# Expert blocks turned by 16-bit DMA transposes in place of TensorE transposes, in a Fourier-filter and top-2 mixture-of-experts kernel

## The chip, the cores and the metric

The kernel runs on one core of a Trainium2 chip. The metric is the time of one execution on the device in microseconds (us): the median of several runs, beside one execution that the hardware profiler recorded. TensorE is called PE in the profile, its weight loads PEld, VectorE DVE, ScalarE ACT, GpSimd POOL and SyncE SP. SP and POOL issue the DMAs.

## The reference

```python
X = np.fft.rfft(x, axis=1)                       # x: 8 x 2496 x 256
y = np.fft.irfft(X * (filt_r + 1j * filt_i)[None], n=2496, axis=1)
x = y.reshape(19968, 256)
noisy = x @ w_gate + np.log1p(np.exp(x @ w_noise)) * noise      # 8 experts
top2 = np.argpartition(-noisy, 2, axis=1)[:, :2]
top2_w = softmax over the two chosen values (sum + 1e-9 below)
for e in range(8):
    for k in range(2):
        mask = top2[:, k] == e
        h = np.maximum(x[mask] @ w1[e], 0.0)     # w1: 8 x 256 x 1024
        out[mask] += top2_w[mask, k, None] * (h @ w2[e])    # w2: 8 x 1024 x 256
```

So a filter over the sequence by Fourier transform, and on its result a mixture of eight experts in which each of the 19968 rows goes to two of them.

## The kernel before

**Stages.** The Fourier part (`fft_stream`) works batch by batch and channel half by channel half with small matrix products. For each half, `i2` (L507) takes the filtered rows from PSUM with one ACT copy (L525) and writes them to the DRAM tensor `y`, 256 values and 8 gate weights (264 32-bit words) a row. `gate` and `slots` choose the experts, and `route` writes lists of row numbers per expert to DRAM.

**Blocks.** The expert part (`expert`, L1070) takes those rows in blocks of one expert. The constants give 16 single blocks of 512 rows (2 after the first batch, 10 more after the second, 4 more after the third), then 24 pairs of 512-row blocks that share their weights, then 7 single blocks of 512, 14 of 256 and 4 of 128: 71 blocks of 512 and 18 small ones. `ready` is the number of batches whose rows a block may hold, so it is 1 for the first two blocks and above 1 for all others.

**One block.** `gather` (L988) has POOL fetch 128 rows at a time from `y` by an indirect DMA into a slot `xg`; there are 8 slots, two 512-row blocks, in the tile `stage`. `turn` (L1001) transposes them on PE: for each half `kc` of the 256 channels up to four 128x128 transposes (L1010) into one PSUM bank `xps`; ACT then copies the bank, rounded, to `mxh` (L1014) and DVE subtracts that from the bank to give the rest, `mxl` (L1015). POOL copies the block's gate weights out of the same slots (L1019). The first layer runs over eight tiles `f` of 128 hidden units, each from six 128x512 matmuls (L122 to L124: high x high, high x low, low x high for both `kc`); the PSUM bank of every third tile is one of `yps`, of the others one of `hps`. ACT applies relu with rounding to `hh` (L1097), DVE makes the rest `hl` (L1098). The second layer goes over the block's quarters `t` of 128 rows (L1122, L1123; earlier blocks L122 to L124 with yps), ACT and DVE scale the result with the gate into one of six slots `yo` (L1127, L1129), and POOL adds it to `out` with an indirect DMA (L1130).

**Weights.** `front` (L969) starts a new expert's block: `load_w` has SP load the eight pieces of w1 and w2 into four slots `wst`, and `wsplit` (L1059 on ACT, L1060 on DVE) splits each into high and low parts. `front` ends with `turn` for its block.

**Order.** Two blocks are held in `ahead`, gathered early by `fetch` (L1063). The next block's `turn` or `front` is written between the first and the second layer of the present block; after each step `run` lets the Fourier stream make some steps, by a table of paces (`PACE`). A scheduler orders the instructions of each engine by a simulated timeline, so that the layers of two blocks and the Fourier products are interleaved; each engine then takes its queue in order. `pin` holds some instructions to the written order, and `after` puts one behind another.

Of the kernel before, what the change touches and what calls it, by code (L numbers as in the profile page):

```python
# [10 lines left out]
F32 = mybir.dt.float32  # L11
R32 = mybir.dt.float32r
F16 = mybir.dt.float16
I32 = mybir.dt.int32
AF = mybir.ActivationFunctionType
ALU = mybir.AluOpType
AX = mybir.AxisListType
# [5 lines left out]
NG = 22  # L23
# [103 lines left out]
def f32v(ap):  # L127
    return ap.bitcast(F32)
# [14 lines left out]
class Moe:  # L143
    def __init__(self, ctx, tc, io):
        self.tc, self.nc, self.io = tc, tc.nc, io
        nc = self.nc
        self.cp = ctx.enter_context(tc.tile_pool(name="cp", bufs=1))
        self.dp = ctx.enter_context(tc.tile_pool(name="dp", bufs=1, space=DRAM))
        self.y = self.dp.tile([NROW, YW], F32, name="y")
# [33 lines left out]
    def setup(self):  # L183
# [12 lines left out]
        self.sgn = cp.tile([64, 20], F32, name="sgn")  # L196


        self.stage = cp.tile([128, 2048 + 8 * YW + 1536], F32, name="stage")
# [29 lines left out]

    def slot(self, nm):  # L230

        at, n, w = {"wst": (0, 4, 512), "xg": (2048, 8, YW), "yo": (2048 + 8 * YW, 6, 256)}[nm]
        i = self.turns[nm] = (self.turns.get(nm, -1) + 1) % n
        return self.stage[:, at + w * i:at + w * i + w]

# [42 lines left out]
    def init_dram(self):  # L278
        nc, io = self.nc, self.io
        z = self.z  # L280

        nc.sync.dma_start(self.lst.rearrange("(n r) c -> n (r c)", r=4), io["empty"].to_broadcast([NLR // 4, 4 * LR]))
        for a, w in (self.y, YW), (io["out"], D):
# [168 lines left out]
    def logits(self, r):  # L452
        nc, P = self.nc, self.P
        if r == 0:
            self.uh = P.tile([120, 24, 16], R32, name="uh")
# [51 lines left out]
    def i2(self, n, g0):  # L507
        nc, P, h = self.nc, self.P, n % 2
        Dh, Dl = self.cD
        th, tl = self.t3t.pop((n, g0))  # L510
        k = min(4, NG - g0)
        m = 128 * k
        p = self.ps("q6")
        if tl is None:
            nc.tensor.matmul(p[:RP, :m], self.rD, th[:120, :m], start=True, stop=True)  # L515
        else:
            nc.tensor.matmul(p[:RP, :m], Dh, th[:120, :m], start=True, stop=False)
            nc.tensor.matmul(p[:RP, :m], Dh, tl[:120, :m], start=False, stop=False)
            nc.tensor.matmul(p[:RP, :m], Dl, th[:120, :m], start=False, stop=True)
# [5 lines left out]
        nc.scalar.copy(yt[:, :k, :128], p[:RP, :m].rearrange("p (g d) -> p g d", g=k))  # L525
# [3 lines left out]
        nc.sync.dma_start(y[:, g0:g0 + k, h * 128:h * 128 + w], yt[:, :k, :w])  # L529

    def fft_stream(self):

# [185 lines left out]
    def gate(self, bt, lgp):  # L718
# [30 lines left out]

        m, c, oh = [], [], []  # L750
        for i in range(2):
            mi, ci, oi = t(f"m{i}", [RP, NG]), t(f"c{i}", [RP, NG]), t(f"oh{i}")
# [213 lines left out]
        nc.gpsimd.tensor_copy(ids, t)  # L966
        return ids, n, nt, s, self.tabs[i]

    def front(self, blk, xg, fill=None):  # L969


        nc = self.nc
        lt, n, nt, s, tabi, ready = blk
        with self.after(self.spw):
            re = nc.sync.value_load(tabi[0:1, 1, s:s + 1], min_val=0, max_val=E - 1)
        self.ra = nc.gpsimd.value_load(tabi[0:1, 1, s:s + 1], min_val=0, max_val=E - 1)
# [5 lines left out]
        if fill and self.held_any:  # L982
            xT = self.pin(self.turn, xg, nt, hold=False, only=[self.nc.tensor.engine])
        else:
            xT = self.turn(xg, nt)
        return w1, xT, w2st

    def gather(self, blk, i):  # L988

        lt, n, nt, s, tabi, ready = blk  # L990
        xg = []
        for t in range(nt):
            x = self.slot("xg")
            self.pin(lambda: self.nc.gpsimd.indirect_dma_start(  # L994
                out=x, out_offset=None, in_=self.y[:BLK + ready * ROWS],
                in_offset=bass.IndirectOffsetOnAxis(ap=lt[:, i, t:t + 1], axis=0)),
                hold=False, only=[self.nc.gpsimd.engine])
            xg.append(x)
        return xg, self.turns["xg"] + 1 - nt

    def turn(self, xg, nt):  # L1001

        nc, P = self.nc, self.P
        xT = []
        xg, at = xg
        w = 128 * nt
        for kc in range(2):
            q = self.PS.tile([128, 512], F32, name="xps", bufs=1)
            for t in range(nt):
                nc.tensor.transpose(q[:, t * 128:(t + 1) * 128], xg[t][:, kc * 128:(kc + 1) * 128], self.ident)  # L1010
            h = P.tile([128, 512], R32, name=f"mxh{kc}", bufs=1)
            l = P.tile([128, 512], R32, name=f"mxl{kc}", bufs=1)
            h, l = h[:, :w], l[:, :w]
            nc.scalar.copy(h, q[:, :w])  # L1014
            nc.vector.tensor_sub(l, q[:, :w], f32v(h))  # L1015
            xT.append((h, l))
        gate = P.tile([128, 4, 1], F32, name="gt", bufs=3)[:, :nt]
        rows = self.stage[:, 2048:2048 + 8 * YW].rearrange("p (s w) -> p s w", w=YW)[:, at:at + nt, D:]
        nc.gpsimd.tensor_copy(gate, rows[:, :, bass.ds(self.ra, 1)])  # L1019
        xT.append(gate)  # L1020
        return xT

    def load_w(self, re, nm, nt):
# [39 lines left out]
    def fetch(self, may):  # L1063

        if len(self.ahead) < 2 and may():
            p = next(self.parts, None)
            if p is not None:
                self.ahead.append((*p, self.gather(*p)))

    def expert(self, parts, may, fill=None):  # L1070

        nc, P = self.nc, self.P
        self.parts, self.ahead = parts, []
        self.fetch(lambda: True)
        cur = None
        while self.ahead:
            blk, i, xg = self.ahead.pop(0)
            lt, n, nt, s, tabi, ready = blk
            w = 128 * nt
            if cur is None:  # L1080
                cur = self.front(blk, xg, fill)
            w1, xT, w2st = cur
            if i == 0:
                w2, adds = [], []
            ids, gate = lt[:, i], xT[2]
            self.fetch(may)
            hh = []
            for f in range(8):

                p = self.PS.tile([128, 512], F32, name="hps", tag="hps" if f % 3 < 2 else "yps", bufs=2)[:, :w]  # L1090
                for kc in range(2):
                    wh, wl = w1[f // 2]
                    o = (f % 2) * 128
# [1 line left out]
                h = P.tile([128, 512], R32, name="hh", bufs=8)[:, :w]  # L1095
                l = P.tile([128, 512], R32, name="hl", bufs=8)[:, :w]
                nc.scalar.activation(h, p, AF.Relu)  # L1097
                nc.vector.scalar_tensor_tensor(l, p, 0.0, f32v(h), op0=ALU.max, op1=ALU.subtract)  # L1098
# [5 lines left out]
            if late:  # L1104
                self.fetch(lambda: True)
            if self.ahead:
                b2, i2, x2 = self.ahead[0]
                cur = (w1, self.turn(x2, nt), None) if i2 else self.front(b2, x2, fill if late else None)
            self.fetch(may)
            yield  # L1110
            for t in range(nt):
# [135 lines left out]
```

## Time and profile before

| | us |
|---|---|
| median of 3 runs | 2302.6 |
| lowest and highest | 2300.22, 2303.27 |
| the profiled execution | 2311.56 |
| its span, first to last instruction | 2309.8 |

The mean granted TensorE clock of the profiled execution was 0.940. Indirect gathers (128 rows of `y` each) took a median of 2.9 us from issue to landing, the scatters 4.2 us. In all 332.80 MB were moved at a mean of 144 GB/s.

In the profile's rows, a group is a line, engine and operation with its tiles; behind the bar stand its busy time, the mean time of one in ns, and how long the engine was idle ahead of it, with what ended that. A row of the timeline is the start, the duration and the instruction; "x4" says that four were merged, and the duration is then that of all. A row of the stages is a stretch of the span with the busy time of each engine in it. A row of waits says who waited for whom: total us, times, longest.

### The profile page before, as it was taken

The numbers are of one execution on the slowest core, as the hardware profiler recorded it, in microseconds if no ns is written. First come the engines' busy times: TensorE is split into PE (matmuls) and PEld (weight loads), VectorE is DVE, ScalarE is ACT, GpSimd is POOL, SyncE is SP. The second block draws the span as 40 slices with busy tenths as digits, with TensorE's granted clock in tenths as the row PEclk, the third lists the DMA queues.
The fourth block names the chain that finished last, engine by engine and source line by source line (L and its number), as shares of the span: only waits on it lengthen the run. The fifth ranks groups of instructions, "written<-read, shape, count | busy, mean of one in ns | idle before, by whom it ended". The sixth has DMA issues, their size and how long they took to land.

```text
span 2309.8 us, 39448 instructions
## 1 busy us (share of the span) xinstructions
PE 2267.6 (98%) x13087; PEld 1898.6 (82%) x13087; DVE 1544.5 (67%) x3356; ACT 1193.7 (52%) x2385; POOL 925.1 (40%) x821
## 2 busy tenths in 40 slices
PE   8889999999999999999999999999999999999998
PEld 6548888888888788887888888888888888889997
DVE  4767788678779665875659655964444444657886
ACT  5655655555664554444544444444434444546775
POOL 4014244334234333443344433435454444444442
PEclk8889999999999999999999999999999999999998
DMA  8686757657765655454544554444444444658774
GB/s 233 181 255 167 184 147 202 170 157 177 192 168 131 148 131 124 102 144 118 117 115 105 138 141 85 90 99 89 97 91 90 89 99 104 149 138 232 218 214 131
DMA packets 286296, 332.80 MB, mean 144 GB/s; under 512 B 37532, under 2 KB 197252, under 8 KB 286084
## 3 DMA queue, kind: packets, MB, share of 16 engines
q1 hardware_dynamic: 224771, 245.80, 35.4%
q0 software_dynamic: 61312, 84.40, 21.9%
q8 instruction: 105, 1.72, 0.3%
q14 instruction: 108, 0.88, 0.1%
HBM read 225.63 MB, written 105.25 MB: 143 GB/s over the span
## 4 chain that ended last, share of the span: by engine, by line
PE 93%; DVE 2%; DMA 2%; ACT 1%; issue 1%; SPq 0%; POOL 0%; POOLq 0%; DVEq 0%; ACTq 0%
PE yps L1122 20%; PE hps L122 13%; PE hps L123 12%; PE hps L124 12%; PE yps L1123 10%; PE xps L1010 3%; PE q L429 3%; PE yps L124 2%; PE yps L122 2%; PE yps L123 2%; PE q L493 2%; PE u L440 1%; PE q L318 1%; PE q L515 1%; PE q L390 1%
## 5 line engine op out<-in xcount | busy, mean ns | idle before, releaser
L1122 PE MATMUL yps<-w,hh 128*128 128x512 f32 x2016 | 715.3, 399 | 0.6 <-DVE stage L1129 0.6
L1130 POOL DMA_INDIRECT out<-stage,ids x316 | 524.6, 1660 | 274.2 <-DVE stage L1129 109.8
L994 POOL DMA_INDIRECT stage<-y,ids x316 | 325.3, 1029 | 665.3 <-PE xps L1010 276.0
L1123 PE MATMUL yps<-w,hl 128*128 128x256 f32 x2016 | 547.2, 281 | 0.2 <-DVE hl L1098 0.2
L123 PE MATMUL hps<-mxl,w1h 128*128 128x512 f32 (+2 forms) x1424 | 534.0, 376 | 0.0
L1098 DVE SCALAR_TENSOR_TENSOR hl<-hps,hh 128x512 fp32r<-128x512 f32 (+2 forms) x712 | 435.8, 626 | 143.4 <-ACT hh L1097 141.6
L124 PE MATMUL hps<-mxh,w1l 128*128 128x512 f32 (+2 forms) x1424 | 526.7, 371 | 0.0
L122 PE MATMUL hps<-mxh,w1h 128*128 128x512 f32 (+2 forms) x1424 | 524.6, 378 | 0.9 <-DVE hl L1098 0.8
L1097 ACT ACTIVATE hh<-hps 128x512 fp32r<-128x512 f32 (+2 forms) x712 | 378.9, 550 | 237.0 <-PE hps L124 226.9
L1122 PEld LDWEIGHTS yps<-w,hh 128*128 128x128 f32 x2016 | 372.3, 188 | 78.4 <-DVE stage L1129 0.9
L1123 PEld LDWEIGHTS yps<-w,hl 128*128 128x128 f32 x2016 | 379.6, 189 | 18.7 <-DVE mxl L1015 1.2
L124 PEld LDWEIGHTS hps<-mxh,w1l 128*128 128x128 f32 x1424 | 268.6, 189 | 45.6
L122 PEld LDWEIGHTS hps<-mxh,w1h 128*128 128x128 f32 x1424 | 265.4, 188 | 48.9 <-DVE hl L1098 2.9
L123 PEld LDWEIGHTS hps<-mxl,w1h 128*128 128x128 f32 x1424 | 268.6, 189 | 40.5 <-issue 0.3
L1127 ACT ACTIVATE stage<-yps,gt 128x256 f32<-128x256 f32 x316 | 142.5, 476 | 268.9 <-PE yps L1123 242.7
L1129 DVE SCALAR_TENSOR_TENSOR stage<-yps,gt,stage 128x256 f32<-128x256 f32 x252 | 115.4, 479 | 177.3 <-ACT stage L1127 177.0
L1015 DVE TENSOR_TENSOR mxl<-xps,mxh 128x512 fp32r<-128x512 f32 (+2 forms) x178 | 112.1, 630 | 147.4 <-ACT mxh L1014 144.9
L1014 ACT CAST mxh<-xps 128x512 fp32r<-128x512 f32 (+2 forms) x178 | 95.8, 538 | 220.3 <-PE xps L1010 186.9
L1059 ACT CAST w1h<-stage 128x512 fp32r<-128x512 f32 x188 | 116.7, 621 | 93.0 <-PE hps L123 56.6
L1060 DVE TENSOR_TENSOR w1l<-stage,w1h 128x512 fp32r<-128x512 f32 x188 | 129.1, 687 | 45.1 <-ACT w1h L1059 44.4
L1060 DVE TENSOR_TENSOR w<-stage,w 128x512 fp32r<-128x512 f32 x224 | 147.0, 685 | 15.0 <-ACT w L1059 14.7
L122 PE MATMUL yps<-w,hh 128*128 128x256 f32 x512 | 146.8, 289 | 2.6 <-ACT hh L1097 2.6
(222 smaller groups left out, 3067.8 us busy)
## 6 DMA issues: line engine op xcount, KB each, us to landing
stage<-w SPq DMA_DIRECT2D x412, 256.0 KB
x<-x SPq DMA_DIRECT2D x88, 256.0 KB
fd<-c SPq DMA_DIRECT2D x77, 240.0 KB
wb<-w SPq DMA_DIRECT2D x18, 1024.0 KB
fx<-fd SPq DMA_DIRECT2D x140, 128.0 KB
out<-z SPq DMA_DIRECT2D x24, 702.0 KB
y<-yt SPq DMA_DIRECT2D x40, 248.6 KB
y<-yt SPq DMA_DIRECT2D x40, 234.0 KB
```

Source lines behind the costliest of these rows:

```text
L122: nc.tensor.matmul(o, lh, rh, start=start, stop=False)
L123: nc.tensor.matmul(o, lh, rl, start=False, stop=False)
L124: nc.tensor.matmul(o, ll, rh, start=False, stop=stop)
L994: self.pin(lambda: self.nc.gpsimd.indirect_dma_start(out=x, out_offset=None, in_=self.y[:BLK + ready * ROWS], in_offset=bass.IndirectOffse ...
L1059: nc.scalar.copy(h, sv)
L1060: nc.vector.tensor_sub(l, sv, f32v(h))
L1097: nc.scalar.activation(h, p, AF.Relu)
L1098: nc.vector.scalar_tensor_tensor(l, p, 0.0, f32v(h), op0=ALU.max, op1=ALU.subtract)
L1122: nc.tensor.matmul(bank, h, hl, start=(f == 0), stop=False)
L1123: nc.tensor.matmul(p, l, hl[:, 0], start=False, stop=(f == 7))
L1127: nc.scalar.activation(o, p, AF.Copy, scale=gate[:, t])
L1130: a = nc.gpsimd.indirect_dma_start(out=self.io["out"][:BLK + ready * ROWS], out_offset=bass.IndirectOffsetOnAxis(ap=ids[:, t:t + 1], axis= ...
```

## The change

`y` becomes an integer tensor of the same size. The ACT copy in `i2` now splits each 32-bit value into its two 16-bit halves, so that within each 128 channels a row of `y` holds 128 low halves and then 128 high halves. Gate weights stay as they are.

512-row blocks with `ready` above 1 are turned by DMA: `flip` issues one `dma_start_transpose` from SP for each 128 gathered rows, 128 x 512 halves, into one tile `xt` (one buffer), and then has POOL copy the gate weights (`take`). Only one turned block stands at a time; the next one's `flip` comes at the end of the present one's `turn` or right behind its gather. `turn` then has DVE join the two halves of each channel (a copy of 1024 16-bit elements for each `kc`) into a 32-bit slot `x32`, ordered behind the fifth tile's subtraction of L1098; ACT's `mxh` and DVE's `mxl` are made from that slot.

All other blocks are turned on PE as before, with an ACT copy ahead that joins the halves from the `xg` slots into `x32`.

To make room, `xg` has 4 slots in place of 8, `yo` 4 in place of 6; `uh` and `oh` share buffers with `ut0` and `gl`. For blocks that are turned by DMA, every third tile of the first layer takes the bank `xps` in place of one of `yps`. `fetch` at the start of a block is only called if the next one is turned, or fewer than four slots are held. The core of the diff:

```diff
-        at, n, w = {"wst": (0, 4, 512), "xg": (2048, 8, YW), "yo": (2048 + 8 * YW, 6, 256)}[nm]
+        at, n, w = {"wst": (0, 4, 512), "xg": (2048, 4, YW), "yo": (2048 + 4 * YW, 4, 256), "x32": (3072 + 4 * YW, 2, 512)}[nm]
...
-        nc.scalar.copy(yt[:, :k, :128], p[:RP, :m].rearrange("p (g d) -> p g d", g=k))
+        nc.scalar.copy(yt.bitcast(U16)[:, :k, :256].rearrange("p g (two d) -> p g two d", two=2),
+                       p.bitcast(U16)[:RP, :2 * m].rearrange("p (g d two) -> p g two d", g=k, two=2))
...
+    def by_dma(self, ent):
+        return ent[0][2] == BLK // 128 and ent[0][5] > 1
+
+    def take(self, ent):
+        xg, at, ra = ent[2]
+        gate = self.P.tile([128, 4, 1], F32, name="gt", bufs=3)[:, :len(xg)]
+        self.nc.gpsimd.tensor_copy(gate, self.picked(ent)[:, :, D:][:, :, bass.ds(ra, 1)])
+        return gate
+
+    def flip(self):
+        ent = next((e for e in self.ahead if not e[3]), None)
+        if ent is None or not self.by_dma(ent) or self.standing:
+            return
+        self.standing = True
+        xt = self.P.tile([128, 4, 512], U16, name="xt", bufs=1)
+        for t, x in enumerate(ent[2][0]):
+            self.nc.sync.dma_start_transpose(xt[:, :, 128 * t:128 * t + 128], x.bitcast(U16)[:, :2 * D])
+        ent[3] = xt, self.take(ent)
...
-    def turn(self, xg, nt):
+    def turn(self, ent):
...
+        if self.by_dma(ent):
+            self.flip()
+        q, xT = [], []
         for kc in range(2):
-            q = self.PS.tile([128, 512], F32, name="xps", bufs=1)
-            for t in range(nt):
-                nc.tensor.transpose(q[:, t * 128:(t + 1) * 128], xg[t][:, kc * 128:(kc + 1) * 128], self.ident)
...
+            x = self.slot("x32")[:, :w]
+            xu = x.bitcast(U16)
+            if ent[3]:
+                with self.after(self.early_l):
+                    nc.vector.tensor_copy(xu.rearrange("p (t two) -> p two t", two=2), ent[3][0][:, 2 * kc:2 * kc + 2])
+            else:
+                nc.scalar.copy(xu.rearrange("p (t d two) -> p t d two", t=nt, two=2),
+                               self.picked(ent).bitcast(U16)[:, :, 256 * kc:256 * kc + 256].rearrange("p t (two d) -> p t d two", two=2))
+            q.append(x)
+        for kc in range(2):
+            x = q[kc]
+            if not ent[3]:
+                x = self.PS.tile([128, 512], F32, name="xps", bufs=1)[:, :w]
+                for t in range(nt):
+                    nc.tensor.transpose(x[:, t * 128:(t + 1) * 128], q[kc][:, t * 128:(t + 1) * 128], self.ident)
+            h = P.tile([128, 512], R32, name=f"mxh{kc}", bufs=1)[:, :w]
+            l = P.tile([128, 512], R32, name=f"mxl{kc}", bufs=1)[:, :w]
+            nc.scalar.copy(h, x)
+            nc.vector.tensor_sub(l, x, f32v(h))
+            xT.append((h, l))
...
+        self.flip()
         return xT
...
-            self.fetch(may)
+            if not self.ahead or self.ahead[0][3] or sum(len(a[2][0]) for a in self.ahead) < 4:
+                self.fetch(may)
+            third = ("xps", 1) if self.by_dma(ent) else ("yps", 2)
...
-                p = self.PS.tile([128, 512], F32, name="hps", tag="hps" if f % 3 < 2 else "yps", bufs=2)[:, :w]
+                tag, bufs = ("hps", 2) if f % 3 < 2 else third
+                p = self.PS.tile([128, 512], F32, name="hps", tag=tag, bufs=bufs)[:, :w]
...
+                v = nc.vector.scalar_tensor_tensor(l, p, 0.0, f32v(h), op0=ALU.max, op1=ALU.subtract)
+                if f == 4:
+                    self.early_l = v
```

More of the change, by code (lines that the diff above doesn't have):

```diff
@@ L14 @@
 I32 = mybir.dt.int32
+U16 = mybir.dt.uint16
 AF = mybir.ActivationFunctionType
@@ L148, in __init__ @@
         self.dp = ctx.enter_context(tc.tile_pool(name="dp", bufs=1, space=DRAM))
-        self.y = self.dp.tile([NROW, YW], F32, name="y")
+        self.y = self.dp.tile([NROW, YW], I32, name="y")
         self.lst = self.dp.tile([NLR, LR], F32, name="lst")
@@ L196, in setup @@
         self.sgn = cp.tile([64, 20], F32, name="sgn")
-        self.stage = cp.tile([128, 2048 + 8 * YW + 1536], F32, name="stage")
+        self.stage = cp.tile([128, 4096 + 4 * YW], F32, name="stage")
         self.turns = {}
@@ L282, in init_dram @@
         nc.sync.dma_start(self.lst.rearrange("(n r) c -> n (r c)", r=4), io["empty"].to_broadcast([NLR // 4, 4 * LR]))
-        for a, w in (self.y, YW), (io["out"], D):
+        for a, w, z in (self.y, YW, z.bitcast(I32)), (io["out"], D, z):
             nc.sync.dma_start(a[:BLK].rearrange("(p r) d -> p r d", p=128),
@@ L454, in logits @@
         if r == 0:
-            self.uh = P.tile([120, 24, 16], R32, name="uh")
+            self.uh = P.tile([120, 24, 16], R32, name="uh", tag="ut0", bufs=1)
             self.ul = P.tile([120, 24, 16], R32, name="ul")
@@ L528, in i2 @@
         y = self.y[BLK + n // 2 * ROWS:BLK + (n // 2 + 1) * ROWS].rearrange("(p g) d -> p g d", p=RP)
-        nc.sync.dma_start(y[:, g0:g0 + k, h * 128:h * 128 + w], yt[:, :k, :w])
+        nc.sync.dma_start(y[:, g0:g0 + k, h * 128:h * 128 + w], yt.bitcast(I32)[:, :k, :w])
     def fft_stream(self):
@@ L751, in gate @@
         for i in range(2):
-            mi, ci, oi = t(f"m{i}", [RP, NG]), t(f"c{i}", [RP, NG]), t(f"oh{i}")
+            mi, ci = t(f"m{i}", [RP, NG]), t(f"c{i}", [RP, NG])
+            oi = P.tile(sh, F32, name=f"oh{i}", tag=("gl", "oh1")[i], bufs=1)
             v.tensor_reduce(mi, nz, axis=AX.X, op=ALU.max)
@@ L967, in read_list, with front @@
         return ids, n, nt, s, self.tabs[i]
-    def front(self, blk, xg, fill=None):
+    def front(self, ent, fill=None):
         nc = self.nc
-        lt, n, nt, s, tabi, ready = blk
+        lt, n, nt, s, tabi, ready = ent[0]
         with self.after(self.spw):
             re = nc.sync.value_load(tabi[0:1, 1, s:s + 1], min_val=0, max_val=E - 1)
-        self.ra = nc.gpsimd.value_load(tabi[0:1, 1, s:s + 1], min_val=0, max_val=E - 1)
         w1st = self.load_w(re, "w1", nt)
@@ L981, in front @@
             fill()
-        if fill and self.held_any:
-            xT = self.pin(self.turn, xg, nt, hold=False, only=[self.nc.tensor.engine])
+        if fill and self.held_any and not self.by_dma(ent):
+            xT = self.pin(self.turn, ent, hold=False, only=[self.nc.tensor.engine])
         else:
-            xT = self.turn(xg, nt)
+            xT = self.turn(ent)
         return w1, xT, w2st
     def gather(self, blk, i):
+        nc = self.nc
         lt, n, nt, s, tabi, ready = blk
+        if i == 0:
+            self.ra = nc.gpsimd.value_load(tabi[0:1, 1, s:s + 1], min_val=0, max_val=E - 1)
         xg = []
@@ L993, in gather @@
             x = self.slot("xg")
-            self.pin(lambda: self.nc.gpsimd.indirect_dma_start(
-                out=x, out_offset=None, in_=self.y[:BLK + ready * ROWS],
+            self.pin(lambda: nc.gpsimd.indirect_dma_start(
+                out=x.bitcast(I32), out_offset=None, in_=self.y[:BLK + ready * ROWS],
                 in_offset=bass.IndirectOffsetOnAxis(ap=lt[:, i, t:t + 1], axis=0)),
-                hold=False, only=[self.nc.gpsimd.engine])
+                hold=False, only=[nc.gpsimd.engine])
@@ L998, in gather, with picked @@
             xg.append(x)
-        return xg, self.turns["xg"] + 1 - nt
-    def turn(self, xg, nt):
+        return xg, self.turns["xg"] + 1 - nt, self.ra
+    def by_dma(self, ent):
+        return ent[0][2] == BLK // 128 and ent[0][5] > 1
+    def picked(self, ent):
+        xg, at, ra = ent[2]
+        return self.stage[:, 2048:2048 + 4 * YW].rearrange("p (s w) -> p s w", w=YW)[:, at:at + len(xg)]
+    def take(self, ent):
+        xg, at, ra = ent[2]
+        gate = self.P.tile([128, 4, 1], F32, name="gt", bufs=3)[:, :len(xg)]
+        self.nc.gpsimd.tensor_copy(gate, self.picked(ent)[:, :, D:][:, :, bass.ds(ra, 1)])
+        return gate
@@ L1005, in turn @@
-        xg, at = xg
+        xg = ent[2][0]
+        nt = len(xg)
         w = 128 * nt
+        if self.by_dma(ent):
+            self.flip()
+        q, xT = [], []
         for kc in range(2):
-            q = self.PS.tile([128, 512], F32, name="xps", bufs=1)
-            for t in range(nt):
[L1010 to L1015, printed above, removed]
-            xT.append((h, l))
@@ L1017, in turn @@
[L1017 to L1020, printed above, removed]
+            x = self.slot("x32")[:, :w]
[6 more added lines that the diff above has]
+                               self.picked(ent).bitcast(U16)[:, :, 256 * kc:256 * kc + 256].rearrange("p t (two d) -> p t d two", two=2))
@@ L1021, in turn @@
+        if ent[3]:
+            self.standing = False
+        else:
+            ent[3] = None, self.take(ent)
+        xT.append(ent[3][1])
+        self.flip()
         return xT
@@ L1067, in fetch @@
             if p is not None:
-                self.ahead.append((*p, self.gather(*p)))
+                self.ahead.append([*p, self.gather(*p), None])
+                self.flip()
     def expert(self, parts, may, fill=None):
         nc, P = self.nc, self.P
-        self.parts, self.ahead = parts, []
+        self.parts, self.ahead, self.standing, self.early_l = parts, [], False, None
         self.fetch(lambda: True)
@@ L1076, in expert @@
         while self.ahead:
-            blk, i, xg = self.ahead.pop(0)
+            if cur is None:
+                cur = self.front(self.ahead[0], fill)
+            ent = self.ahead.pop(0)
+            blk, i = ent[:2]
             lt, n, nt, s, tabi, ready = blk
             w = 128 * nt
-            if cur is None:
-                cur = self.front(blk, xg, fill)
             w1, xT, w2st = cur
@@ L1106, in expert @@
             if self.ahead:
-                b2, i2, x2 = self.ahead[0]
-                cur = (w1, self.turn(x2, nt), None) if i2 else self.front(b2, x2, fill if late else None)
+                e2 = self.ahead[0]
+                cur = (w1, self.turn(e2), None) if e2[1] else self.front(e2, fill if late else None)
             self.fetch(may)
```

2 lines of the change are left out of this document (removed).

## The prediction

> **What bounds the kernel now.** I read the head of the page first, with the shares and the chain of work that ended last.
>
> ```profile
> span 2309.8 us, 39448 instructions
> PE 2267.6 (98%) x13087; PEld 1898.6 (82%) x13087; DVE 1544.5 (67%) x3356; ACT 1193.7 (52%) x2385; POOL 925.1 (40%) x821
> PE 93%; DVE 2%; DMA 2%; ACT 1%; issue 1%; SPq 0%; POOL 0%; POOLq 0%; DVEq 0%; ACTq 0%
> PE yps L1122 20%; PE hps L122 13%; PE hps L123 12%; PE hps L124 12%; PE yps L1123 10%; PE xps L1010 3%; PE q L429 3%; PE yps L124 2%; PE yps L122 2%; PE yps L123 2%; PE q L493 2%; PE u L440 1%; PE q L318 1%; PE q L515 1%; PE q L390 1%
> ```
>
> TensorE is the bound, and the transposes of line 1010 hold 3% of the chain. A busy PE need not be one without slack, so I then cut the span into stages (columns: stretch, length, busy time of PE, PEld, DVE, ACT, POOL; clock; DMA share; GB/s), and asked the same stages for line 1015 alone, which runs twice per block.
>
> ```profile
> 173.00:577.00 404.00, 398.02 (x2622) 349.27 (x2620) 316.03 (x682) 231.62 (x453) 159.26 (x137) 0.95 0.67 172
> 577.00:1500.00 923.00, 922.16 (x5178) 767.42 (x5177) 648.41 (x1378) 456.25 (x888) 369.48 (x311) 0.95 0.54 128
> 1500.00:2100.00 600.00, 600.00 (x3140) 505.85 (x3140) 308.49 (x587) 261.39 (x503) 272.98 (x246) 0.95 0.48 109
> 2100.00:2310.00 210.00, 199.54 (x1421) 185.33 (x1420) 163.10 (x346) 142.38 (x345) 88.68 (x89) 0.93 0.70 194
> ...
> 173.00:577.00 404.00, 17.89 (x26) 0.95 0.67 172
> 577.00:1500.00 923.00, 44.07 (x64) 0.95 0.54 128
> 1500.00:2100.00 600.00, 35.43 (x52) 0.95 0.48 109
> ```
>
> Between 577 and 2100 us PE is idle for under 1 us, at a clock of 0.95. The others differ by stage: before 577 us DVE is busy for 316 of 404 us (78%) and the DMA engines for 67%; after 1500 us for 51% and 48%. So PE time saved is worth most late and least before 577 us. A block takes 923/32 = 28.8 us in the second stage, 600/26 = 23.1 us in the third.
>
> **What the transposes cost PE.** The group says 102.6 us, but its spans overlap their neighbours; the price is what they add between the neighbours' starts.
>
> ```profile
> L1010 PE MATMUL xps<-ident,stage 128*128 128x128 f32 x632 | 102.6, 276 | 9.5 <-DMA stage<-y,ids 7.9 <-DVE mxl L1015 1.4 <-DVE hl L1098 0.2
> ...
> 131.88 0.47 PE L1010 MATMUL xps<-ident,stage 128*128 128x128 f32 x1 [4.61 <-DMA stage<-y,ids]
> 134.25 0.48 PE L1010 MATMUL xps<-ident,stage 128*128 128x128 f32 x1 [1.89 <-DMA stage<-y,ids]
> ...
> 1814.00 0.62 PE L1122 MATMUL yps<-w,hh 128*128 128x512 f32 x2
> 1814.46 0.60 PE L1010 MATMUL xps<-ident,stage 128*128 128x128 f32 x4
> 1814.82 0.48 PE L123 MATMUL hps<-mxl,w1h 128*128 128x512 f32 x1
> 1815.14 0.39 PE L124 MATMUL hps<-mxh,w1l 128*128 128x512 f32 x1
> 1815.62 0.40 PE L122 MATMUL hps<-mxh,w1h 128*128 128x512 f32 x1
> 1815.85 0.40 PE L123 MATMUL hps<-mxl,w1h 128*128 128x512 f32 x1
> ```
>
> 128x512 matmuls start 0.23 us apart (1814.00 to 1814.46 for two, 1815.62 to 1815.85 for one). Without the transposes, 1814.46 to 1815.14 would be one such step; it is 0.68. Four transposes cost 0.45 us, a block's eight 0.90. The chain agrees: 3% of 2309.8 is 69 us for 632, 0.11 each.
>
> The code gives 71 blocks of 512 rows; the first two (one batch ready) stay with PE. 69 x 0.90 = **62 us** of PE go. The other 80 transposes stay, and so do the waits for gathers (4.61 and 1.89 us), which fall on the first block.
>
> **What DVE gets.** Two joins per turned block, each of 1024 16-bit elements; and the subtraction of line 1015 reads SBUF twice.
>
> ```profile
> L1098 DVE SCALAR_TENSOR_TENSOR hl<-hps,hh 128x512 fp32r<-128x512 f32 x568 | 383.0, 686 | 132.4 <-ACT hh L1097 130.7
> L1060 DVE TENSOR_TENSOR w1l<-stage,w1h 128x512 fp32r<-128x512 f32 x188 | 129.1, 687 | 45.1 <-ACT w1h L1059 44.4
> L1015 DVE TENSOR_TENSOR mxl<-xps,mxh 128x512 fp32r<-128x512 f32 x142 | 97.9, 690 | 140.1 <-ACT mxh L1014 138.9
> L1098 DVE SCALAR_TENSOR_TENSOR hl<-hps,hh 128x256 fp32r<-128x256 f32 x112 | 44.4, 418 | 7.4 <-ACT hh L1097 7.4
> L345 DVE COPY stage<-q 128x480 f32<-128x480 f32 x5 | 3.3, 658 | 12.0 <-PE q L341 12.0
> ```
>
> The subtraction costs the same from SBUF (687 against 690 ns). 256 more elements cost 268 ns, so 1024 cost 686 + 2 x 268 = 1.22 us at one element per cycle, and 0.69 if two go at once. The only copy in the trace (480 elements, 658 ns) goes at one, so I take 1.22: 168 us for 138 joins. [...] After 577 us even 1.22 is covered: 648 + 64 x 1.22 = 726 of 923 us, and 308 + 52 x 1.22 = 372 of 600. Before 577 us there are (1 + 26 - 4)/2 = 11.5 turned blocks (one line-1015 instruction lies earlier, four are of PE's blocks); with them DVE is busy for 344 of some 394 us, 87%, fuller in places, and the DMA engines fill up as well. There I take the gain, 11.5 x 0.90 = **10 us, as lost** (bounds: 0, and 20 if stalls cost as much again).
>
> **The transposing DMAs.** Four per block on SP's queue, 128 x 512 halves, 131,072 bytes each. No row shows one.
>
> ```profile
> q1 hardware_dynamic: 224771, 245.80, 35.4%
> stage<-y,ids POOLq DMA_INDIRECT x316, 2.9
> 1509.47 0.37 SPq L529 DMA_DIRECT2D y<-yt  x1
> 1795.13 0.96 POOL L994 DMA_INDIRECT stage<-y,ids  x1 [0.30 <-issue]
> 1796.40 0.96 POOL L994 DMA_INDIRECT stage<-y,ids  x1 [0.30 <-issue]
> ```
>
> The hardware queue's packets take 0.354 x 16 x 2309.8 us / 224771 = 58 ns, at 1094 bytes. As such packets a transfer takes 120 x 58 ns / 16 = 0.4 us; in runs of 32 bytes (16 elements), 4096 x 58 / 16 = 14.8 us. The destination is cut into 128 columns, 256 bytes of a source row, so I take 512 x 58 / 16 = 1.9 us, 7.4 a block, and about 10 to landing (2.9 behind a gather). Who waits: the transposes stand on SP behind the gather and the previous block's joins, and weights, FFT input and y stand behind them; DVE's joins stand in front of the relu subtractions; and POOL's next gather, which has four slots where it had eight, waits until they are read, with the scatters behind it. A round of the four slots is four gathers (3 x 1.27 + 0.96 + 2.9 = 7.7 us) and the turn (10): 17.7 us, below the 23.1 - 0.9 = 22.2 of a late block. **Covered**, until the turn takes 22.2 - 7.7 = 14.5 us. The DMA share, 48% late, gains 7.4/22.2 = 33 points.
>
> [...]
>
> **ACT, opening and tail.**
>
> ```profile
> L525 ACT COPY yt<-q 117x512 f32<-117x512 f32 x80 | 46.9, 586 | 31.4 <-PE q L519 22.1 <-PE q L515 7.6 <-DMA fd<-c 0.4
> L525 ACT COPY yt<-q 117x256 f32<-117x256 f32 x16 | 6.0, 378 | 2.4 <-PE q L519 1.9 <-PE q L515 0.3
> L1059 ACT CAST w<-stage 128x512 fp32r<-128x512 f32 x224 | 132.8, 631 | 7.8 <-PE yps L124 3.4 <-PE yps L1123 2.5
> PE q L515 <- ACT yt L525: 2.9, 4, 1.0
> ACT th L380 <- DMA fx<-fd: 19.0, 6, 5.0
> ```
>
> A y copy moves 1024 elements instead of 512: 208 ns per 256 more, so +0.42 us, 96 times. 24 of them (four channel halves of six) are in the opening, where PE waited for ACT there only 2.9 us in all: I take **3 us** of 0 to 10. The first block's gather was waited for, so its ACT join (631 + 416 = 1.05 us) shows: **1 us**. In the tail 14 + 4 small blocks get two ACT joins each ahead of PE's transposes, at most 14 x 1.26 + 4 x 0.84 = 21 us if uncovered; ACT is free for 68 of 210 us: **4 us** of 0 to 21. ACT waited for FFT input in six places (19 us), with little margin; SP's new waits cost **2 us** of 0 to 20. Six scatter slots become four: a scatter must land within four of a late block's quarters (5.8 us each), so nothing. PSUM's third bank for the first layer, the shared u buffers and the moved gate copies (same count) I cost at nothing: no wait of PE for them is in its list of waits. They would cost what appears there.
>
> Sum: 62 - 10 - 3 - 1 - 4 - 2 = 42 us off the profiled execution, whose own time is 2311.56 (span 2309.8). The runs' median is 2302.6, 9 us less; the same 42 off it gives **2261**.
>
> **Rivals.**
> - Full gain, all covered: 2302.6 - 62 = 2240. For it: no PE wait after 577 us. Against: DVE at 87% before that.
> - No change: the 138 joins stall DVE where the transposes stood, 0.45 us each: 62 us given back, 2303. For it: engines take their work in order, and a join waits for a DMA. Against: it stands behind the fifth subtraction, half a block later than its data, by my estimate.
> - Slower, the turn as pace: over 14.5 us the ring of four slots sets the third stage's period. Each us more costs 26 us there (the second stage, 27.9 us a block, bears 20.2). The gain is gone at 14.5 + 42/26 = 16.1 us, 4.0 per transfer, twice my estimate. At 18 us: 2261 + 26 x 3.5 = 2352. For it: bounds from 0.4 to 14.8 per transfer; early DMA share.
> - Slower, pieces in series: 16 pieces of 128x128 a block, one after another, each between SP's 0.37 us and a landing's 2.9; the geometric middle, 1.04, gives 16.6 us a turn: 2261 + 26 x 2.1 = 2316. For it: all stand on one queue. Against: SP's other DMAs overlap. [...]
>
> **How the numbers follow.** Forecast 0.56 (its own range 2242 to 2290), full gain 0.10, no change 0.08, turn as pace 0.16, pieces in series 0.10. Faster 0.66, same 0.08, slower 0.26; 0.2%, 4.6 us, is about what a measurement can tell. The range, 2236 to 2360, holds all but the dearer part of the slow cases.
>
> **What would show it.** In the profile after: line 1010 x80; joins x138, at 1.22 or 0.69 us; 276 transposing DMAs, and the time to landing of one; late blocks 22.2 us apart; DVE near 90% before 577 us. Wrong, if PE's list of waits shows the joins' subtractions late by microseconds per block, if gathers wait for transposes over the whole late stage, or if weights or fx land late behind SP's transposes.

## The result and the profile after

| | us |
|---|---|
| before, median of 4 runs (lowest, highest) | 2302.71 (2300.22, 2303.27) |
| after, median of 4 runs (lowest, highest) | 2264.2 (2263.34, 2265.61) |
| after, the profiled execution, and its span | 2265.61, 2263.8 |
| ratio after to before, 95% interval | 0.9835, 0.9818 to 0.9852 |

The change took off 38.5 us in the medians. The forecast was 2261, 42 us less; its range was 2236 to 2360. The head of the page after, its chain and its busiest DMA queue (packets, MB, share of 16 engines' span; before 224771, 245.80, 35.4%):

```profile
span 2263.8 us, 39149 instructions
PE 2202.2 (97%) x12535; PEld 1839.7 (81%) x12535; DVE 1622.2 (72%) x3494; ACT 1238.0 (55%) x2425; POOL 954.5 (42%) x821
PE 69%; DVE 1%; issue 1%; ACT 0%; DMA 0%; POOL 0%; POOLq 0%; ACTq 0%; DVEq 0%
q1 hardware_dynamic: 374915, 282.01, 45.8%
```

PE is still the bound. It has 552 matmuls fewer: 69 blocks of eight transposes. DVE gained 138 instructions, two joins a block. The stages, cut like those of before but for the last border; then one stretch each of the changed kernel and of a second profile of the kernel before, for the subtraction alone (line 1061, before 1015):

```profile
173.00:577.00 404.00, 398.91 (x2575) 351.27 (x2574) 324.73 (x675) 237.85 (x459) 165.48 (x139) 0.99 0.81 191
577.00:1500.00 923.00, 913.57 (x5001) 754.71 (x4999) 700.46 (x1488) 478.52 (x905) 391.58 (x318) 0.99 0.67 149
1500.00:2050.00 550.00, 549.79 (x2799) 460.87 (x2798) 322.51 (x618) 247.23 (x479) 270.51 (x232) 1.00 0.63 135
2050.00:2264.00 214.00, 203.61 (x1447) 188.43 (x1445) 167.07 (x352) 161.49 (x384) 92.35 (x92) 0.98 0.70 193
...
1574.00:1932.05 358.05, 22.04 (x32) 1.00 0.61 123
...
1596.00:1966.20 370.20, 22.13 (x32) 1.00 0.45 98
```

Late, PE stays full. The last two rows are the same sixteen blocks in both kernels (the 51st to the 66th, beside which nothing of the Fourier part runs): 370.2 us before and 358.05 after, 23.14 and 22.38 a block; the forecast said 22.2. Before 577 us PE is no emptier than it was (398.91 of 404 against 398.02). But the second stage, in which PE was idle for 0.84 us, now shows 9.4 us. That loss was not in the forecast. Most of it, 7.7 us, lies in one place:

```profile
600.00:650.00 50.00, 42.29 (x232) 32.92 (x232) 32.91 (x69) 26.98 (x53) 17.89 (x17) 0.90 0.79 196
```

The granted clock of these 50 us is 0.90, where the stages around are at 0.99 to 1.00, so PE lost here both by waiting (idle for 7.7 us) and by a slower clock (0.50 to 0.52 between 622.2 and 632 us, where 128x512 matmuls come 0.43 us apart in place of 0.23). The new and changed groups, and the transposing DMAs (x, then shortest, median and longest issue in ns on SP):

```profile
L1047 DVE COPY stage<-xt 128x1024 uint16<-128x1024 uint16 x138 | 96.8, 755 | 0.1
L1061 DVE TENSOR_TENSOR mxl<-stage,mxh 128x512 fp32r<-128x512 f32 x138 | 94.6, 686 | 16.0 <-ACT mxh L1060 15.2
L526 ACT COPY yt<-q 117x1024 uint16<-117x1024 uint16 x80 | 81.2, 1015 | 36.1 <-PE q L520 28.4 <-PE q L516 5.2 <-DMA y<-yt 1.8
L1049 ACT COPY stage<-stage 128x512 uint16<-128x512 uint16 x28 | 19.3, 688 | 0.5 <-DVE mxl L1061 0.5
L1057 PE MATMUL xps<-ident,stage 128*128 128x128 f32 x80 | 16.1, 283 | 0.0
...
L1030 SPq DMA_TRANSPOSE xt<-stage x276: 1189/1222/3861, 200.2 to 2000.2; - x138
```

The joins take 0.755 us, and DVE hardly ever waited ahead of one (0.1 us in all): the transposed data were always there. The subtraction costs 686 ns from SBUF, as forecast. A transpose holds SP's issue for 1.22 us. What it takes of the 16 DMA engines follows from queue q1: (0.458 x 2263.8 - 0.354 x 2309.8) x 16 / 276 engine-us, that is 0.79 us of all 16 per transpose, if nothing else on that queue changed its cost.

One turn of a late block, from the timeline after:

```profile
1813.87 1.16 POOL L1018 COPY gt<-stage 128x4 f32 x1
1814.23 1.43 DVE L1047 COPY stage<-xt 128x1024 uint16<-128x1024 uint16 x2
1815.68 5.15 SPq L1030 DMA_TRANSPOSE xt<-stage  x4
1818.91 1.02 POOL L999 DMA_INDIRECT stage<-y,ids  x1 [3.88 <-DMA xt<-stage]
...
1823.24 0.95 POOL L999 DMA_INDIRECT stage<-y,ids  x1 [0.30 <-issue]
```

DVE joins one block (1814.23 to 1815.66); right behind it, as `xt` is free, SP issues the next block's four transposes in 5.15 us, and 3.2 us after the first of them POOL may refill that slot. The last of the four refills is issued by 1824.19, 10 us after the first join began, of the block's 22.

### The profile page after: what moved, and what is told of

Its sections match the earlier page's. It is cut to its first block, busy times and chain, and to the rows that moved or that the text cites. A ratio compares the mean times of both kernels' runs of the same rounds, so it can differ in the third digit from the quotient of the medians.

```text
span 2263.8 us, 39149 instructions
## 1 busy us (share of the span) xinstructions
PE 2202.2 (97%) x12535; PEld 1839.7 (81%) x12535; DVE 1622.2 (72%) x3494; ACT 1238.0 (55%) x2425; POOL 954.5 (42%) x821
## 4 chain that ended last, share of the span: by engine, by line
PE 69%; DVE 1%; issue 1%; ACT 0%; DMA 0%; POOL 0%; POOLq 0%; ACTq 0%; DVEq 0%
PE yps L1177 20%; PE hps L123 11%; PE hps L124 10%; PE yps L1178 10%; PE hps L125 10%; PE q L430 1%; PE q L494 1%; PE u L441 1%; PE q L518 0%; PE q L519 0%; PE q L520 0%; PE q L393 0%; PE q L394 0%; PE q L395 0%; PE xps L1057 0%
## 5 line engine op out<-in xcount | busy, mean ns | idle before, releaser
L1185 POOL DMA_INDIRECT out<-stage,ids x316 | 538.6, 1704 | 447.6 <-DVE stage L1184 223.2
L999 POOL DMA_INDIRECT stage<-y,ids x316 | 333.8, 1056 | 538.4 <-DMA xt<-stage 400.4
L1178 PE MATMUL yps<-w,hl 128*128 128x256 f32 x2016 | 539.0, 282 | 0.0
L123 PE MATMUL yps<-w,hh 128*128 128x256 f32 x512 | 145.2, 286 | 2.8 <-ACT hh L1150 2.4
L124 PE MATMUL yps<-w,hh 128*128 128x256 f32 x512 | 142.6, 284 | 0.0
L1107 ACT CAST w<-stage 128x512 fp32r<-128x512 f32 x224 | 137.6, 637 | 8.9 <-DMA stage<-w 4.8
```

Source lines behind the costliest of these rows:

```text
L123: nc.tensor.matmul(o, lh, rh, start=start, stop=False)
L124: nc.tensor.matmul(o, lh, rl, start=False, stop=False)
L999: self.pin(lambda: nc.gpsimd.indirect_dma_start(out=x.bitcast(I32), out_offset=None, in_=self.y[:BLK + ready * ROWS], in_offset=bass.Indir ...
L1107: nc.scalar.copy(h, sv)
L1178: nc.tensor.matmul(p, l, hl[:, 0], start=False, stop=(f == 7))
L1185: a = nc.gpsimd.indirect_dma_start(out=self.io["out"][:BLK + ready * ROWS], out_offset=bass.IndirectOffsetOnAxis(ap=ids[:, t:t + 1], axis= ...
```

## The experiments

The runs fall into four sessions, each with its own runs of the kernel before: 2300.88 us (first four kernels below), 2310.88 (third bank, small blocks, first two), 2309.7 (the two paces) and 2301.91 (the last three). The changed kernel itself ran beside 2302.71 and, in the last session, beside 2301.91. So where a kernel of the first three sessions is held against it, the comparison crosses sessions; by what is found below, that alone can be worth 5 to 8 us.

**Before, again.** The kernel before, for a profile at the clock of after (the two profiles shown had 0.940 and 0.991).

> The kernel before, once more, for a second profile beside those of the changed kernels of the same chip. The granted clock was 0.940 in the first profile of before and 0.991 in the profile after. If the change makes the clock rise, it is about 0.94 here again; if the clock is a matter of the chip or the hour, it can be 0.99. Either way the time should be 2300 to 2312 us, since 128x512 matmuls start 0.23 us apart at both clocks.

2304.28 us at a granted clock of 0.993, against 2311.56 at 0.940. The clock in the records is not the change's doing.

```profile
PE 2252.3 (98%) x13087; PEld 1889.8 (82%) x13087; DVE 1543.4 (67%) x3356; ACT 1193.9 (52%) x2385; POOL 928.6 (40%) x821
...
600.00:650.00 50.00, 50.00 (x324) 43.20 (x323) 35.97 (x56) 33.91 (x65) 19.45 (x17) 1.00 0.72 185
```

In the 50 us in which the changed kernel stalls, this one has a full PE. Its span is 2302.5, so 38.7 us are to be explained. I took from both timelines, for each step from one matmul's start to the next, what it is longer than in a packed stream (0.231 us for 512 columns, 0.1155 for 256, 0.1125 for 128, a transpose among them, the few others in proportion to 512). Missing records count as excess too, in both alike:

| stretch, us | before again | after |
|---|---|---|
| 0 to 173 | 76.6 | 82.0 |
| 173 to 600 | 19.6 | 17.9 |
| 600 to 650 | -0.1 | 14.2 |
| 650 to 1500 | 15.3 | 16.9 |
| 1500 to 2050 | 3.9 | 7.5 |
| 2050 to the end | 6.6 | 6.9 |

After loses 5.4 more in the opening and 18.1 behind it, 14.3 of that in the one stall; 62.1 (69 blocks of 0.90) less 23.5 is 38.6. The sum has to close, since the excess is all that the steps hold beyond their prices: it tells where the time went, and is no test of the price of a transpose.

**PE turns all.** The new layout of `y`, the ACT joins and the four slots stay; no block is turned by DMA.

> All of the change but the DMA turn: y in planes of halves, four gather slots and four output slots, and every block joined by ACT and transposed by PE. The forecast's theory (the gain is PE's time for 552 transposes) expects the after time plus 62 us plus what 138 joins of 1.05 us on ACT show, so 2320 to 2350 us, slower than before. The rival that the gain comes from the other edits (order, buffers, clock) expects 2290 us or less.

```diff
     def by_dma(self, ent):
-        return ent[0][2] == BLK // 128 and ent[0][5] > 1
+        return False
```

2366.5 us (2361.37 to 2370.82), ratio 1.0291 (1.0274 to 1.0308): over 16 us more than expected. The page's head, two groups and one row of ACT's waits:

```profile
PE 2271.5 (96%) x13087; PEld 1894.5 (80%) x13087; DVE 1538.8 (65%) x3356; ACT 1376.4 (58%) x2563; POOL 922.4 (39%) x821
...
L1049 ACT COPY stage<-stage 128x1024 uint16<-128x1024 uint16 x142 | 165.1, 1169 | 201.9 <-DMA stage<-y,ids 181.3 <-PE yps L1178 10.2 <-PE q L395 6.3
L1057 PE MATMUL xps<-ident,stage 128*128 128x128 f32 x632 | 101.2, 275 | 5.5 <-ACT stage L1049 5.2
...
ACT stage L1049 <- DMA stage<-y,ids: 181.3, 58, 7.4
```

PE's busy time is 69 us above the changed kernel's (2271.5 against 2202.2), and its idle time, span less busy, 26 us (88 against 62); together the 95.7 us by which the two spans differ (the medians, of two sessions, differ by 102). Here a join waits for a gather; by the code, four slots no longer let a gather come a block ahead. The layout without the DMA transposes is 66 us worse than the kernel before (2300.88): the joins and the fewer slots are a price, which the transposes repay.

**Every transpose twice.**

> Each of the 276 DMA transposes is issued a second time into the same place, the second four behind the first four, each waiting for its first. SP then issues eight of 1.22 us for a block, so a turn takes about 12 to 14 us in place of some 7. The forecast's theory (covered until a turn takes 14.5 us) expects no more than 10 us over the time after, 2264 to 2275. The rival that the turn already sets the pace expects 5 us or more per block in the last 25 blocks at least, 2390 us or more.

```diff
-        for t, x in enumerate(ent[2][0]):
+        for t, x in list(enumerate(ent[2][0])) * 2:
```

2279.0 us (2276.7 to 2282.7), ratio 0.9901 (0.9885 to 0.9918): 15 us above the changed kernel of another session. That is more than the 10 expected by about what a session can shift, and far from what a turn that sets the pace would cost. Rows of this kernel, issues and three stretches:

```profile
q1 hardware_dynamic: 525059, 318.22, 55.7%
...
L1030 SPq DMA_TRANSPOSE xt<-stage x552: 1188/1218/3527, 203.2 to 2023.3; - x184
...
300.00:400.00 100.00, 97.78 (x660) 87.36 (x659) 88.75 (x217) 56.99 (x112) 54.58 (x39) 1.00 0.94 202
400.00:577.00 177.00, 171.86 (x1095) 150.73 (x1095) 131.86 (x282) 103.87 (x202) 72.38 (x61) 0.99 0.94 202
...
700.00:2050.00 1350.00, 1346.05 (x7089) 1117.45 (x7088) 928.08 (x1930) 652.68 (x1248) 631.94 (x514) 1.00 0.76 161
```

After 700 us PE is as full as with single transposes (1346.05 of 1350; changed kernel 1348.07). The loss is mostly earlier, where the DMA engines stood at 0.81 already and now stand at 0.94: from 400 to 577 us PE is idle for 5.1 us instead of 0.4, over 173 to 577 us for 11.5 instead of 5.1. The extra 276 give 0.85 us of 16 engines each, by the same working as above, close to the 0.79.

**Every join twice.**

> Each of the 138 joins on DVE (0.75 us) is done twice, 103 us more work on DVE. The forecast's theory (joins are covered after 577 us, and matter for 11.5 blocks before) expects at most 11.5 x 1.5 = 17 us more than after, 2264 to 2282. The rival that joins stand in the way of the relu subtractions expects a good part of 103 us, 2320 us or more.

```diff
-                with self.after(self.early_l):
-                    nc.vector.tensor_copy(...)
+                for _ in range(2):
+                    with self.after(self.early_l):
+                        nc.vector.tensor_copy(...)
```

2280.34 us (2278.81 to 2282.84), ratio 0.9908 (0.9892 to 0.9925): 16 us above the changed kernel of another session, for 97 us more of DVE's time. The joins here, and one stretch of this kernel, then of the changed one:

```profile
L1048 DVE COPY stage<-xt 128x1024 uint16<-128x1024 uint16 x276 | 194.2, 751 | 0.3 <-DMA xt<-stage 0.2
...
300.00:400.00 100.00, 91.62 (x578) 78.40 (x577) 88.73 (x222) 52.75 (x102) 41.61 (x36) 0.97 0.73 173
```
```profile
300.00:400.00 100.00, 98.06 (x650) 87.38 (x649) 92.63 (x229) 58.12 (x114) 47.99 (x36) 0.98 0.81 182
```

From 300 to 400 us DVE is busy for 93% already in the changed kernel. There the second join costs PE: idle for 8.4 us instead of 1.9. Of 8.0 us of PE's listed waits there, 7.1 end on DVE's work, 3.0 of them on the relu subtractions, for which the changed kernel has no such wait. From 700 to 2050 us PE is idle for 4.3 us instead of 1.9, with 106 of the 138 extra joins in that stretch. So DVE holds PE up in that one stretch with 1.5 us per turn half, and hardly with 0.755.

**Third bank back, and again.** The third tile of the first layer in `yps`, as it was. First in the second session, then beside the changed kernel in the last.

> Only the PSUM bank of every third first-layer tile goes back to yps for blocks that are turned by DMA. The forecast's theory (the gain is PE's time; the bank was costed at nothing) expects 2264 us within 5. The rival that the free bank xps is what keeps PE fed expects 2275 us or more, with PE's first layer waiting for the output's readers.

```diff
-            third = ("xps", 1) if self.by_dma(ent) else ("yps", 2)
+            third = ("yps", 2)
```

2281.72 us (2276.25 to 2285.37), ratio 0.987 (0.9849 to 0.9891). Held against 0.9835 that looked like a bank worth 8 us.

> Third tile of the first layer in a bank of yps again, for the blocks turned by DMA; this time beside the changed kernel on one chip. If the extra bank is worth what the first comparison across chips gave, it is 6 to 10 us slower than the changed kernel; if the forecast's price of nothing holds, it lies within 4 us of it.

2262.76 us (2259.12 to 2267.31), ratio 0.9836 (0.982 to 0.9851), with the changed kernel at 2264.45 beside it. The bank is worth nothing that can be measured here, and the first reading compared across sessions what does not compare.

**Small blocks too.** Blocks of 256 rows turned by DMA as well; 56 more transposes leave PE.

> The 14 blocks of 256 rows are turned by DMA too: 56 transposes (6.3 us of PE) and 28 ACT joins go, 28 half-size DVE joins come. The theory that PE's time is the gain wherever the turn is covered expects 2255 to 2261 us. The rival that a small block's 11 us is too short for gather and turn in one ring of slots expects 2268 us or more, with PE waiting after 2050 us.

```diff
-        return ent[0][2] == BLK // 128 and ent[0][5] > 1
+        return ent[0][2] > 1 and ent[0][5] > 1
...
-                    nc.vector.tensor_copy(..., ent[3][0][:, 2 * kc:2 * kc + 2])
+                    nc.vector.tensor_copy(..., ent[3][0][:, 2 * kc:2 * kc + 2, :w])
```

2273.39 us (2271.95 to 2274.83), ratio 0.9836 (0.982 to 0.9853). The changed kernel did not run in that session; the one with its third bank back did, and equals it in the last session. Against that one, at 2281.72, this is 8 us faster, as expected (3 to 9). So it probably beats the changed kernel, by a comparison with one step in between.

**The first two blocks too.**

> The first two blocks are turned by DMA too: 16 transposes (1.8 us) and four ACT joins go. The first block's gather is on the path, and behind it come four DMA transposes of 1.2 us each with their landing and two DVE joins, where PE transposed each 128 rows as they came. The theory of uncovered latency expects 2266 to 2274 us; the rival that PE's time is all that counts expects 2261 us.

```diff
-        return ent[0][2] == BLK // 128 and ent[0][5] > 1
+        return ent[0][2] == BLK // 128
```

2283.99 us (2279.34 to 2287.09), ratio 0.9881 (0.9862 to 0.99). The first scatter comes at 195.45 us, 7 and 10 later than in the other two kernels of that session (188.5 and 185.4), so the turn of the first block is not covered. Against the same neighbour (2281.72) the whole kernel is only 2 us slower, which these runs do not separate from nothing.

**Two other paces.** To bring the Fourier stream forward at the stall.

> The change with the pace of the second set at 230 in place of 200, so that the Fourier stream makes more steps beside its ten blocks. After loses some 15 us of PE time between 600 and 650 us, where the gathers of the fourth batch wait for the last y writes of that batch, 33 us later than before. If the late Fourier stream is the cause, the loss falls to 5 us or less there and the time is 0.5% lower than after's 0.9835 of before: 0.977 to 0.980. The rival that four gather slots or SP's queue make the stall expects 0.983 to 0.985.

> The change with the pace of the third set at 65 in place of 60: a twelfth more Fourier steps beside its four blocks only. If the late Fourier stream makes the stall, a few microseconds of the 15 go: 0.980 to 0.983 of before. The rival expects 0.983 to 0.985.

```diff
-PACE = {0: 110, 1: 200, 2: 60}
+PACE = {0: 110, 1: 230, 2: 60}
```

2277.02 us (2273.01 to 2278.34), ratio 0.9858 (0.984 to 0.9876); the other, with 65 for the third set, 2277.36 (2275.43 to 2283.95), 0.9863 (0.9843 to 0.9882). The stall stayed, 12.8 and 14.5 us by starts. These kernels can tell nothing of its cause: the scheduler gave both the same order of instructions on every engine as the changed kernel has. They are two more measurements of that kernel, in a session with 2309.7 us for before, and show what a ratio can move by from session to session: 0.0023 and 0.0028. A pace of 80 for the third set, the stronger form of this question, has no time on record.

**After, again.**

> The changed kernel itself, as the measure for the other two on the same chip. The two kernels with other paces issue the same instructions in the same order on every engine as the changed kernel does, so their ratios of 0.9858 and 0.9863 are two more measurements of it, beside 0.9835. I expect 0.9835 to 0.9865. If it comes out at 0.986, what I put down to the third bank (0.987) and to the first two blocks (0.9881) shrinks to 2 and 5 us, and turning the small blocks by DMA (0.9836) would be a gain of some 5 us.

2264.45 us (2262.26 to 2267.16), ratio 0.9837 (0.9825 to 0.985).

**The Fourier part first.** An order that the scheduler has to keep.

> The first-layer matmuls of the last three single blocks of the third set are put behind the last inverse-transform matmul written so far, so that on TensorE the fourth batch's last inverse transform stands behind 1878 matmuls of the expert part instead of 2160 (kernel before: 1942). Theory: the stall at 600 to 650 us is there because the fourth batch's rows and list come too late, behind expert blocks that run ahead. Then its 15 us fall to under 5, the fourth batch's last y copy comes 40 to 60 us earlier than in the changed kernel, the first gather of the pairs is issued before the third set's last block ends, and the time falls by 8 to 14 us. Rival: the switch itself (new weights, list, gather, turn, one behind the other with four slots) costs the 15 us; then the y copies come sooner and the stall stays within 4 us of what it was. A third way: the denser Fourier stretch makes PE wait for its ACT and DMA work and gives the 10 us back before 600 us.

```diff
-            nc.tensor.matmul(p[:RP, :m], Dl, th[:120, :m], start=False, stop=True)
+            self.lasti = nc.tensor.matmul(p[:RP, :m], Dl, th[:120, :m], start=False, stop=True)
...
-                    _mm3(nc, p, wh[:, kc, o:o + 128], ...)
+                    with self.after(self.lasti if f == 0 and kc == 0 and ready == 3 and s >= 13 else None):
+                        _mm3(nc, p, wh[:, kc, o:o + 128], ...)
```

2315.79 us (2313.08 to 2318.93), ratio 1.0063 (1.005 to 1.0076): 51 us slower than the changed kernel, a time that none of the three ways had. A row of its stages, one of PE's waits over the whole execution (2.3 us in the changed kernel), and one of POOL's timeline:

```profile
540.00:690.00 150.00, 108.65 (x619) 84.59 (x618) 117.13 (x305) 71.23 (x131) 26.95 (x22) 0.81 0.58 151
...
PE ra L926 <- DVE oc L922: 21.4, 7, 8.6
...
580.52 1.47 POOL L945 DMA_INDIRECT lst<-ro,row  x1 [19.96 <-DVE new L867]
```

The list did come 26 us sooner (606.24 in the changed kernel), and the fourth batch's last copy into `yt` 25 us sooner (594.77 against 619.43), not the 40 to 60 expected. But the edit went too far: the first layer of the fourteenth block waited for part of the fifth batch as well, and starts at 636.82. From 540 to 690 us PE, with the Fourier part and its routing almost alone, is idle for 41 us. This is the third way, four times as dear as I had put it: without expert blocks beside it, the Fourier part leaves PE idle; the run does not decide what the stall of the changed kernel comes from.

## Where the stall is, as far as the traces tell

The timelines of PE, ACT, POOL and SP in the changed kernel around it, and two of SP's waits from 595 to 630 us. Of the single blocks, the fifteenth has its last matmul at 608.78; the sixteenth, counted by its scatters, begins at 624.34:

```profile
607.73 0.40 PE L327 MATMUL q<-xh,hl 117*120 117x512 f32 x1
...
608.78 0.28 PE L125 MATMUL yps<-w,hl 128*128 128x256 f32 x1
...
620.07 0.50 PE L393 MATMUL q<-th,hl 128*128 128x512 f32 x1 [2.75 <-ACT yt L526]
...
624.34 0.79 PE L123 MATMUL hps<-mxh,w1h 128*128 128x512 f32 x1
624.93 0.63 PE L124 MATMUL hps<-mxl,w1h 128*128 128x512 f32 x1
625.36 0.63 PE L123 MATMUL hps<-mxh,w1h 128*128 128x512 f32 x1
...
627.34 0.80 PE L123 MATMUL hps<-mxh,w1h 128*128 128x512 f32 x1 [0.93 <-ACT w1h L1107]
...
632.04 0.40 PE L123 MATMUL hps<-mxh,w1h 128*128 128x512 f32 x1
632.27 0.39 PE L124 MATMUL hps<-mxl,w1h 128*128 128x512 f32 x1
```
```profile
609.01 0.59 ACT L362 COPY c<-q 120x512 f32<-120x512 f32 x1
...
606.24 1.47 POOL L945 DMA_INDIRECT lst<-ro,row  x1 [0.30 <-DVE sge L877]
```
```profile
598.79 0.38 SPq L305 DMA_DIRECT2D x<-x  x1
609.62 0.32 SPq L363 DMA_DIRECT2D fd<-c  x1
...
613.75 0.42 SPq L963 DMA_DIRECT2D lt<-lst  x1
614.27 1.34 SPq L531 DMA_DIRECT2D y<-yt  x1
...
618.56 0.42 SPq L963 DMA_DIRECT2D lt<-lst  x1
...
620.20 0.35 SPq L1079 DMA_DIRECT2D stage<-w  x1
...
SPq L363 <- ACT yt L529: 10.5, 1, 10.5
SPq L305 <- DVE xl L324: 6.3, 1, 6.3
```

For 15.6 us PE has no expert matmul. The sixteenth block was gathered long before (its last gather at 550.77); what it lacks are its weights, whose casts PE waits for. They are issued at 620.20 at the earliest, and stand on SP's queue behind the Fourier part's transfers, the reading of the list of the pairs and writes of `y`. What held that queue was the Fourier part: it stood for 6.3 us ahead of a load of `x`, and then for 10.5 us ahead of the write of `c`, the Fourier part's intermediate (L363), whose copy ACT ended at 609.60 (the row of waits names the ACT copy right behind it). It could only come behind PE's products of 607.73, which stand among the fifteenth block's last matmuls. The list, written at 606.24, did not hold it: from 609.62 to 620.20 the queue never waits for more than 1.0 us. In the kernel before (second profile) the list was written at 572.80 and read at 592.64, the sixteenth block's weights followed from 604.39 on, and PE was full. So the expert part has run ahead of the Fourier part, and SP's one queue turns that into a wait for weights. When PE then starts, its matmuls come 0.43 us apart until 631.35, and 0.23 from 632.04 on. The granted clock goes with that: 0.50 to 0.52 between 622.2 and 632 us, 1.00 between 632 and 650. From 624.34 the slow stretch lasts 7.7 us, with a wait of 0.93 among them; from the end of that wait, at 627.34, it is 4.7. What brought the clock down, and what up again, no run shows.

That this order on SP is the cause is read from the traces; no run put the weights ahead of the Fourier part's transfers, and it stays open how much of the 14 us that would bring.

## Why the prediction was right, and where it was not

- **PE's price, 62 us: right, but not all of it comes off.** In the second profile of before, the 32 sets of four transposes of the sixteen late blocks cost 0.44 us each, where one set had given 0.45. But these blocks got shorter by 0.76 us and not by 0.90 (22.38 for the 22.2 forecast); the account has the rest as 3.6 us more between the steps from 1500 to 2050 us, and no run shows what causes it.
- **The joins: mis-sized.** 0.755 us, not 1.22. That is near the 0.69 that I had worked out as the other value; that two elements go at once is my reading, and no run shows it. The one copy row that I went by moves 32-bit values out of PSUM (480 of them in 658 ns), a join 16-bit values within SBUF (1024 in 755 ns): the wrong neighbour, though no run shows which of the two differences counts.
- **"Before 577 us 10 us lost": wrong in place.** The step failed with the size of the join: DVE stood at 80% there, not 87%, and nothing was lost. The doubled joins show that at 1.5 us something would have been, from 300 to 400 us. In its place came the stall at 600 to 650 us, 14.3 us, which the forecast did not have: I had asked which engine would be full, not which stream would run ahead. The sum held because one loss stood for another, and that is luck.
- **The turn, covered: right, with room.** I took 1.9 us of 16 engines per transpose, measured 0.79, so the DMA share from 1500 to 2100 us rose by 16 points (0.48 to 0.64), not 33. The pieces are not in series with landings: four are issued in 5.15 us, and twice as many leave PE idle for only 4.0 of 1350 us after 700 us (1.9 with single ones). Both slower rivals fall by that. The 14.8 us for runs of 32 bytes rested on a size that no run shows: queue q1 has 150144 packets and 36.21 MB more than before, 544 packets of 241 bytes per transpose on average, at 0.79 x 16 / 544 us, that is 23 ns each, where I had 512 at 58.
- **SP: a part not costed.** The 2 us were for waits behind a transpose; that one holds the queue for 1.22 us, where I had 0.37 for an issue, was not in the sum: 4.9 us a block. It has no direct part in the stall: SP issues no transpose between 576 and 632 us, and the sixteenth block's first weights at 620.20.
- **Gathers do wait for transposes**, 400.4 us in 116 places over the whole kernel, which I had named as a sign of being wrong. It was none: POOL's gathers waited before as well, for PE's transposes (276 us), and from 700 to 2050 us PE is idle for 1.9 us in all.
- **ACT and the opening:** 4 us forecast for the opening (3 + 1). The first scatter comes at 186.3 and 181.7 us in the two profiles of before, at 187.5 and 185.0 in the two of after: 2.3 later on average, so the 5.4 of the account is not sure. The copies of `y` take 1.015 us, as forecast (0.586 + 0.42). **The tail:** 4 us forecast, 0.3 by starts.
- **The bank, at nothing: right,** though one comparison said otherwise for a while.

## What to carry to other kernels

When a change makes one of two interleaved streams faster, look at the places where that stream depends on the other: here the slower one's results came no sooner, and 14.3 us were lost there, far from any edited line, by the traces as a wait for weights on a shared queue. Price a new operation by the row that has its memories and its width, not by the only row of its name, which gave 1.22 us here for what took 0.755. And hold a variant against the changed kernel in the same session: here one ratio moved by 0.0023 to 0.0034 between sessions for the same program or its equal, which is 5 to 8 us, as much as most of the questions were about.

## What the runs showed that was not expected

The granted clock of 0.94 in the first profile, against 0.993 in the second of the same kernel, went with 2311.56 and 2304.28 us, but matmuls of 512 columns came 0.232 us apart in both (median, 700 to 2050 us), and the sixteen late blocks took 23.18 and 23.14 us each: 5% of clock in the records, under 0.2% of pace. A copy of 1024 16-bit elements costs ACT 1.17 us (SBUF to SBUF, joining) and 1.015 (out of PSUM, splitting), DVE 0.755. And in sessions where the kernel before took 2310 us instead of 2302, the changed kernel took 12 to 13 us more, most of it after 2050 us (excess by starts 17 to 19 us instead of 7).
